# Fourth PV of a chunk directly behind gate/up, W2 tiles fetched six ahead, and another order of the first half's output projection

## The chip, the cores and the metric

The kernel runs on one core of a Trainium2 chip. The metric is the time of one execution on the device in microseconds (us). Before the change it is 560.99 us, the median of three runs (560.61, 560.99, 562.88).

## What is computed

Layer normalisation, then attention and a gated feed-forward layer side by side on the same normalised rows, and the sum of both with the input:

```
xn = layernorm(x)                                   # 2048 x 576
q, k, v = heads of xn @ wqkv                        # 32 heads of 18
p = softmax(q k^T / sqrt(18)), key within the 256 last positions
a = (p v) @ wo
h = silu(xn @ w1) * (xn @ w3)                       # 2048 x 4608
out = x + a + h @ w2
```

## The kernel before

The 2048 rows go in four chunks of 512 (`c` = 0 to 3). A chunk has three stages on TensorE.

1. For chunks 1 to 3, nine projection jobs make q, k and v (for chunk 0 they stand ahead of everything).
2. Thirty-six gate/up units (`u` = 0 to 35). Unit `u` makes 128 of the 4608 hidden columns for all 512 rows with 18 matmuls on 64 rows each, nine pairs (`unit_pairs`, line 686). Its up and gate results stand in two banks of PSUM. ScalarE takes tanh of the gate bank (`unit_tanh`, line 695), and VectorE makes the hidden tile in two instructions (`unit_h`): line 701 reads the gate bank, line 704 the up bank. Between units stand the score steps (line 570) with their exponentials on ScalarE (579) and masks on GpSimd (606), spaced by a count of matmul pairs (`clock`, `nxt`), and three of the four PV groups (`pv`, line 627), each for eight heads. VectorE is also given the statistics and the normalisation (lines 371 to 383) of the next chunk's rows; those of its last 128 rows stand at units 33 and 35 (`near`).
3. The W2 stage. The output has two halves of 288 columns. Per half, nine tiles of W2 (512 x 288, 288 KB) are each used by 16 matmuls of 128 rows (line 744), four row tiles `tt` by four `fl`; the four accumulators `ACC[tt]` are PSUM banks. The attention output is projected into the same accumulators: first the remainder, four matmuls on 64 rows (`wr`, line 756), later the others (`wo`, line 750). At the end of half 0, VectorE adds x and stores each accumulator (`out`, line 764), and SP sends it off (766). The order is a list (`p2_list`), its items counted by `n`, which starts at -4 with the four remainder matmuls.

PSUM has eight banks. The units take three pairs in turn, scores the fourth. In the W2 stage the accumulators are the pair of unit 33 and the score pair; the fourth PV group takes the two banks of unit 34, since `ring_of` begins with `jobs[NF - 2]`. Its results go over VectorE (line 636, transposes), a reciprocal (641), a scaling on GpSimd (642), VectorE again (649) and four transfers on SP (`o_pack`, line 674) into `oT`, from which `wo` reads. GpSimd also copies the old keys (`keep_keys`, line 550) at the head of the stage.

The queues work in program order. SP issues most transfers: the gate/up weights (`w13`, three buffers, each filled by six parts of 192 KB, `load_part`, line 323; `owed` hands them out two per unit, each behind a named TensorE instruction), x rows (299), the transposed normalised rows (408), and the exchange of their halves (`xn_swap`, line 415, into `xnS`). ACT's queue issues the W2 tiles (`load_w2`, line 355). There are eight W2 buffers: four of their own, and four (`w2x`) in the gate/up buffer that the last units have read. Tiles 0 to 3 of the next chunk are fetched in the W2 stage of this one (`next_w2`); for chunk 0 they are fetched by SP at units 20, 22, 24 and 26.

The kernel waits by semaphores that a small dependency tracker (`_Prog`) places: a first write to a bank waits for all readers of what stood in it.

Of the kernel before, what the change touches and what calls it, by code (L numbers as in the profile page):

```python
# [164 lines left out]
def bass_parallel_sum__sliding_block__glu_gated_swiglu__prompt_kernel(  # L165
# [18 lines left out]
    NC = S // CH  # L184
    TB = CH // 128
    G = H // 4
    NF = F // 128
    NFC = F // 512
# [9 lines left out]
    with ExitStack() as es:  # L198
# [1 line left out]
        def sb(name, shape, dtype=dt.bfloat16):  # L200
            return es.enter_context(nc.sbuf_tensor(name, shape, dtype))

        NXP, NOF, NPT, NW13, NW2, NOD = 7, 4, 10, 3, 4, 2
        KB, NB, NV = 64, CH // 64, 12
        ident = sb("ident", [128, 128])
        xp = [sb(f"xp{i}", [128, D]) for i in range(NXP)]
# [10 lines left out]
        wo = sb("wo", [128, 5, D])  # L217
        w13 = [sb(f"w13_{i}", [128, 9, 512]) for i in range(NW13)]
        w2 = [sb(f"w2_{i}", [128, 4, HD]) for i in range(NW2)]
# [36 lines left out]
        oT = sb("oT", [128, 5, CH])  # L256
# [26 lines left out]
        def half_bank(b):  # L283
# [5 lines left out]
            out=ident[:], in_=ident[:], compare_op=ALU.not_equal, fill=1.0,  # L289
# [5 lines left out]
        def load_x(t, eng="sp"):  # L295
            nonlocal xp_ctr
            s = xp_ctr % NXP
            xp_ctr += 1
            add(eng, lambda e: e.dma_start(xp[s][:], x2[t * 128:(t + 1) * 128, :]), w=[("xp", s)], dma=f"xp{s}")
            return s  # L300
# [11 lines left out]
        def load_part(after=(), behind=()):  # L312

            nonlocal nfill
            if nfill >= 6 * NC * NFC:
                return
            k, i = divmod(nfill, 6)
            s, dst = w13_at(k)
            part, n = divmod(i, 2)
            c0 = (k % NFC) * 512  # L320
            src = (B_w3, B_w1)[n]
            nfill += 1
            add("sp", lambda e: e.dma_start(
                dst[64 * n:64 * n + 64, 3 * part:3 * part + 3, :],
                src[192 * part:192 * part + 192, c0:c0 + 512].rearrange("(kd p) f -> p kd f", p=64)),
                r=list(behind), after=after, dma=f"w13_{s}_{n}", **{"j" if i else "w": [("w13", s)]})
# [5 lines left out]
        def last_pe():  # L332
            return next(o for o in reversed(P.ops) if o.eng == "pe")
# [6 lines left out]

        w2x = w13[1][:, :, :].rearrange("p a b -> p (a b)")[:, 0:NW2 * 4 * HD].rearrange("p (n k d) -> p n k d", n=NW2, d=HD)

        def w2_at(c, i):
            n = i % (2 * NW2)
            if n < NW2:
                s = (n + 2 * c) % NW2
                return s, w2[s]
            return n, w2x[:, n - NW2, :, :]

        def load_w2(c, i, eng="act", after=()):  # L350
            if c >= NC:
                return
            s, dst = w2_at(c, i)
            half, fc = divmod(i, NFC)
            add(eng, lambda e: e.dma_start(
                dst[:, :, :], B_w2[fc * 512:(fc + 1) * 512, half * HD:(half + 1) * HD].rearrange("(fl p) d -> p fl d", p=128)),
                w=[("w2", s)], after=after, dma=f"w2_{s}")

        def next_w2(c, i):
            if i < 10:  # L360
                load_w2(c, i + 8)
            elif i < 12:
                load_w2(c + 1, i - 10)
            elif i >= 16:
                load_w2(c + 1, i - 14)


        def ln_stats(t, s, part):
# [340 lines left out]
        def p2_list(c):  # L709

            seq = []
            for half in range(2):
                apart = half == 0 or c + 1 < NC
                if half == 0:
                    seq += [("wr", 0, 0, 0, tt, 0, False) for tt in range(TB)]
                for fc in range(NFC):
                    sl = half * NFC + fc
                    edge = fc == NFC - 1 or (half == 1 and fc == 0)
                    pairs = [(fl, tt) for fl in range(4) for tt in range(TB)]
                    if edge:  # L720
                        pairs = [(fl, tt) for tt in range(TB) for fl in range(4)]
                    for n, (fl, tt) in enumerate(pairs):
                        seq.append(("w2", half, fc, fl, tt, sl, n == len(pairs) - 1))
                        if fc == NFC - 1 and fl == 3:
                            seq += [("wo", half, fc, kd, tt, sl, False) for kd in range(4 if apart else 5)]
                            if half == 0 or not apart:
                                seq.append(("out", half, fc, 0, tt, sl, False))
            if c + 1 < NC:
                for what in ("wr", "out"):
                    seq += [(what, 1, 0, 0, tt, 0, False) for tt in range(TB)]  # L730
            return seq
# [3 lines left out]
        def p2_item(c, item, xs):  # L735
            nonlocal of_ctr
            what, half, fc, k, tt, sl, last = item
            d0 = half * HD
            bank = PS[:, ACC[tt], 0:HD]
            key = [("ps", ACC[tt])]  # L740
            if what == "w2":
                f = fc * 4 + k
                buf, wt = w2_at(c, sl)
                add("pe", lambda e: e.matmul(  # L744
                    bank, hT[:, f, tt * 128:(tt + 1) * 128], wt[:, k, :], start=(f == 0 and half == 1), stop=False),
                    r=[("h", f), ("w2", buf)], **{"w" if f == 0 and half == 1 else "j": key})
                if last:
                    next_w2(c, sl)
            elif what == "wo":
                add("pe", lambda e: e.matmul(  # L750
                    bank, oT[:, k, tt * 128:(tt + 1) * 128], wo[:, k, d0:d0 + HD], start=False,
                    stop=(k == (3 if half == 0 else 4))),
                    r=[("oT", j) for j in range(G // 2)] + ["oTz", "wo"], j=key)
            elif what == "wr":
                r0 = 64 * (tt % 2)
                add("pe", lambda e: e.matmul(  # L756
                    bank, oT[r0:r0 + 64, 4, tt * 128:(tt + 1) * 128], wo[r0:r0 + 64, 4, d0:d0 + HD],
                    start=(half == 0), stop=(half == 1), tile_position=(r0, 0)),
                    r=[("oT", 0), "oTz", "wo"], **{"w" if half == 0 else "j": key})
            else:  # L760
                o = of_ctr % NOF
                of_ctr += 1
                t = c * TB + tt
                add("dve", lambda e: e.tensor_tensor(ofin[:, o, :], bank, xp[xs[tt]][:, d0:d0 + HD], ALU.add),  # L764
                    r=key + [("xp", xs[tt])], w=[("of", o)])
                add("sp", lambda e: e.dma_start(out2[t * 128:(t + 1) * 128, d0:d0 + HD], ofin[:, o, :]),
                    r=[("of", o)], dma=f"out{o}")
# [67 lines left out]
        for h in range(2):  # L835
# [9 lines left out]
            for n, (dst, src) in enumerate(moves):  # L845
                dealt.append(add("pool", lambda e, dst=dst, src=src: e.tensor_copy(dst, src),
                                 r=[f"wqk{h}", "wqkd"], **{"j" if n else "w": [f"wp{h}"]}))
# [30 lines left out]
        for c in range(NC):  # L878
# [21 lines left out]
            side = {}  # L900
# [48 lines left out]
            for u in range(NF):  # L949
# [13 lines left out]
                    if n in (3, 8):  # L963
                        owe_part(op)
                unit_tanh(u, b0[0])
                if u % 4 == 3 and u < NF - 4 and (c or u != 15):
                    owed += 6
                if next_pv in pv_ready and clock >= pv_ready[next_pv] and next_pv < 3:
                    j = next_pv
# [38 lines left out]
                if c == 0 and u == 18:  # L1008
# [3 lines left out]
                    for p in range(2):  # L1012
                        add("sp", lambda e, p=p: e.dma_start(wo[64 * p:64 * p + 64, 4, :], rows[:, 2:Dh, :]),
                            j=["wo"], dma="wo")
                if c == 0 and u in (20, 22, 24, 26):
                    load_w2(0, (u - 20) // 2, "sp")
                if u == 29:
                    xs = [load_x(c * TB + tt) for tt in range(TB)]
            assert done == len(att) and next_pv == 3, (done, next_pv)
            ring_of[:] = [*jobs[NF - 2], *jobs[NF - 1]]  # L1020
# [3 lines left out]
            if c + 1 < NC:  # L1024
                for g in range(G):
                    keep_keys(g)
            for i in range(NW2, 2 * NW2):
                load_w2(c, i, after=(last_pe(),))
            banks = ()
            for n, item in enumerate(p2_list(c), -TB):  # L1030
                p2_item(c, item, xs)
                if n == 3:
                    for u in sorted(side):
                        for what in side.pop(u):
                            what()
                elif n == 19:
                    banks = (ring(), ring())
                    pv(c, 3, banks)
                    pv_out(banks[0], 0)
                    pv_out(banks[1], 1)  # L1040
                    o_scale(0)
                    o_turn(6, 0)
                    o_turn(6, 1)
                    o_scale(1)
                    o_turn(7, 0)
                    o_turn(7, 1)
                    o_pack(3, "sp")
                elif n == 40 and c + 1 < NC:
                    xn_send((c + 1) * TB + 3)
                elif n == 300 and c + 1 < NC:  # L1050
                    xn_swap(c + 1, ("sp", "sp"))
                elif n in (100, 120) and c + 2 < NC:
                    t = (c + 2) * TB + (n == 120)
                    xslot[t] = load_x(t)

        with nc.Block() as block:
            P.replay(es, block)
# [28 lines left out]
```

## Time and profile before

| What | Value |
|---|---|
| median of 3 runs | 560.99 us |
| profiled execution, its own time | 560.94 us |
| its span | 559.1 us |
| TensorE matmul busy | 554.5 us (99%) |
| VectorE / ScalarE / GpSimd busy | 311.8 / 253.0 / 163.4 us |
| gate/up matmuls (line 686) | 181.9 + 154.9 us busy |
| W2 matmuls (line 744) | 147.3 us busy, 1152 of them |
| bytes moved by DMA | 85.90 MB, mean 154 GB/s |

The span is the time between the first and the last instruction of the profiled execution. An instruction's row in the order of time has its start in the span, its length, its engine and line, the tiles it writes and reads, and how many of its kind follow one another; square brackets hold the engine's idle time before it and who ended it. A matmul's length includes its way through the array, so that rows of one engine overlap; the distance from start to start is what a matmul costs.

### The profile page before, as it was taken

To read this page: it belongs to the slowest core of one execution; us is meant where nothing else is said; L and a number is where in the kernel's file an instruction comes from. 1 tells how busy PE (TensorE), PEld (TensorE's weight loads), DVE (VectorE), ACT (ScalarE), POOL (GpSimd) and SP (SyncE) were. 2 spreads that over 40 slices of the span, in tenths; PEclk is the share of its full clock that TensorE was granted. 3 is DMA by queue.
4 is the path that set the end of the run, shared out by engine and by line. 5 is a ranking of instruction groups with operands and counts; after the bars stand their busy time and mean duration, and the time that the engine had idled before them with its cause. 6 is when DMAs were issued, how large, how long until landed. Compare 5 with 4: busy or idle time off the path is not lost.

```text
span 559.1 us, 15730 instructions
## 1 busy us (share of the span) xinstructions
PE 554.5 (99%) x6767; PEld 346.9 (62%) x6767; DVE 311.8 (56%) x584; ACT 253.0 (45%) x349; POOL 163.4 (29%) x383
## 2 busy tenths in 40 slices
PE   9999999999999999999999999999999999999998
PEld 4445455677687455477766545547777654555776
DVE  7466788710366778851046668884105567767211
ACT  4357776100286776600037777650004676666000
POOL 6413454400033445330003444533000333433000
PEclk9999999999999999999999999999999999999999
DMA  9998899994366368599325736869913673661730
GB/s 249 206 192 183 186 187 193 213 266 122 86 141 146 89 175 161 138 238 258 86 72 138 167 86 160 162 172 243 228 51 74 137 172 95 150 163 32 203 107 22
DMA packets 127883, 85.90 MB, mean 154 GB/s; under 512 B 35430, under 2 KB 125502, under 8 KB 127814
## 3 DMA queue, kind: packets, MB, share of 16 engines
q1 hardware_dynamic: 89890, 63.17, 50.6%
q10 hardware_dynamic: 37924, 21.73, 16.0%
q8 instruction: 53, 0.87, 0.7%
q14 instruction: 16, 0.13, 0.1%
HBM read 71.37 MB, written 2.36 MB: 132 GB/s over the span
## 4 chain that ended last, share of the span: by engine, by line
PE 95%; DMA 2%; DVE 1%; SPq 0%; POOL 0%; issue 0%
PE ps L686 50%; PE ps L744 23%; PE ps L450 9%; PE ps L570 6%; PE ps L627 4%; PE ps L750 3%; DMA oT<-od 1%; DMA xp<-in_A_x_dram 0%; SPq L674 0%; PE ps L756 0%; DVE xn L383 0%; POOL oq L642 0%; DVE od L649 0%; DVE stats L371 0%; DVE stats L373 0%
## 5 line engine op out<-in xcount | busy, mean ns | idle before, releaser
L686 PE MATMUL ps<-xnT,w 64*128 64x512 bf16 x1400 | 181.9, 376 | 0.0
L686 PE MATMUL ps<-xnS,w 64*128 64x512 bf16 x1120 | 154.9, 376 | 0.0
L744 PE MATMUL ps<-w,hT 128*128 128x288 bf16 x1152 | 147.3, 286 | 0.1
L701 DVE SCALAR_TENSOR_TENSOR gs<-th,ps 128x512 bf16<-128x512 bf16 x144 | 97.8, 680 | 80.3 <-ACT th L695 78.9
L579 ACT ACTIVATE pt<-ps 128x1024 bf16<-128x1024 f32 (+1 forms) x112 | 113.2, 1011 | 63.4 <-PE ps L570 62.4
L744 PEld LDWEIGHTS ps<-w,hT 128*128 128x128 bf16 x1152 | 112.0, 98 | 29.9 <-issue 1.5
L686 PEld LDWEIGHTS ps<-xnT,w 64*128 64x128 bf16 x1400 | 72.5, 94 | 56.3
L606 POOL TENSOR_TENSOR pt<-pt,mk 128x128 int32<-128x128 int32 (+1 forms) x199 | 80.5, 427 | 79.3 <-ACT pt L579 79.3
L704 DVE SCALAR_TENSOR_TENSOR hT<-gs,ps 128x512 bf16<-128x512 bf16 x144 | 98.9, 686 | 5.0
L695 ACT ACTIVATE th<-ps 128x512 bf16<-128x512 f32 x144 | 85.4, 593 | 23.8 <-PE ps L686 23.6
L686 PEld LDWEIGHTS ps<-xnS,w 64*128 64x128 bf16 x1120 | 59.0, 94 | 51.1
L764 DVE TENSOR_TENSOR ofin<-ps,xp 128x288 bf16<-128x288 f32 x32 | 13.8, 454 | 121.9 <-PE ps L750 63.8
L463 ACT ACTIVATE stage<-ps 128x512 bf16<-128x512 f32 x16 | 9.6, 597 | 145.1 <-PE ps L450 142.8
L606 POOL TENSOR_TENSOR hT<-hT,mk 128x128 int32<-128x128 int32 (+1 forms) x31 | 12.4, 422 | 168.5 <-ACT hT L579 168.5
L570 PE MATMUL ps<-qv,kv 64*128 64x320 bf16 (+4 forms) x528 | 53.5, 260 | 0.0
L570 PEld LDWEIGHTS ps<-qv,kv 64*128 64x128 bf16 x528 | 28.0, 94 | 25.1 <-ACT pt L579 0.5
L450 PE MATMUL ps<-xnT,wp 64*128 64x512 bf16 (+1 forms) x360 | 39.0, 355 | 0.0
L579 ACT ACTIVATE stage<-ps 128x1024 bf16<-128x1024 f32 x24 | 24.6, 1024 | 12.6 <-PE ps L570 12.6
L649 DVE STREAM_TRANSPOSE od<-oq 128x256 bf16<-128x256 bf16 x64 | 25.8, 427 | 6.3 <-POOL oq L642 6.3
L450 PEld LDWEIGHTS ps<-xnT,wp 64*128 64x128 bf16 x360 | 20.0, 94 | 13.1
L642 POOL TENSOR_TENSOR oq<-uq,rden 128x288 bf16<-128x288 f32 x16 | 10.8, 674 | 39.0 <-DVE rden L641 39.0
L606 POOL TENSOR_TENSOR stage<-stage,mk 128x128 int32<-128x128 int32 (+1 forms) x42 | 17.0, 423 | 17.3 <-ACT stage L579 17.2
(60 smaller groups left out, 353.0 us busy)
## 6 DMA issues: line engine op xcount, KB each, us to landing
w<-in_B_w_dram SPq DMA_DIRECT2D x210, 192.0 KB, 4.3
w<-in_B_w_dram ACTq DMA_DIRECT2D x68, 288.0 KB, 5.7
xp<-in_A_x_dram SPq DMA_DIRECT2D x29, 144.0 KB, 5.0
out_dram<-ofin SPq DMA_DIRECT2D x32, 72.0 KB, 2.0
xnS<-xnT SPq DMA_DIRECT2D x8, 256.0 KB, 5.2
oT<-od SPq DMA_DIRECT2D x56, 36.0 KB
pt<-in_A_wqkv_dram SPq DMA_DIRECT2D x4, 288.0 KB, 6.5
hT<-in_B_w_dram SPq DMA_DIRECT2D x6, 192.0 KB, 7.3
```

The lines of the kernel that those rows point to most:

```text
L450: op = add("pe", lambda e, out_=out_, st=st, mv=mv, n=n, r0=r0, first=first: e.matmul(out_, st, mv, start=first, stop=(part == 1 and n == ...
L570: add("pe", lambda e, r0=r0, out_=out_, kb=kb, q0=q0, nb=nb: e.matmul(out_, kb4[r0:r0 + 64, g, kb + NV - NB, :] if kb < 0 else kv[r0:r0 + ...
L579: add("act", lambda e: e.activation(pt_slot(sl)[:, 0:w, :], PS[:, SC[0]:SC[1] + 1, 0:w].rearrange("p r q -> p q r"), ACT.Exp, scale=scale) ...
L606: add("pool", lambda e, vb=vb, mm=mm: e.tensor_tensor(vb, vb, mm, ALU.mult), r=(key if n == 0 else []) + ["mk"], **{"w" if n == 0 else "j" ...
L627: add("pe", lambda e, p=p, q=q, pr=pr, sl=sl, g=g, pos=pos, q0=q0, nb=nb, col=col, first=first, n=n: e.matmul(PS[32 * q:32 * q + VW, banks ...
L649: add("dve", lambda e: e.transpose(od[i][:, g % 2, c0:c0 + CH // 2], oq[:, c0:c0 + CH // 2]), r=["oq", "oq0"], **{"j" if half or g % 2 els ...
L686: op = add("pe", lambda e, n=n, r0=r0, r=r, k=k, src=src: e.matmul(PS[:, b0 + r, :], wt[r0:r0 + 64, k, fl * 128:(fl + 1) * 128], src, star ...
L695: add("act", lambda e: e.activation(th[i][:], PS[:, bg, :], ACT.Tanh, scale=0.5), r=[("ps", bg)], w=[("th", i)])
L701: add("dve", lambda e: e.scalar_tensor_tensor(out=gs[i][:], in0=th[i][:], scalar=1.0, in1=PS[:, bg, :], op0=ALU.add, op1=ALU.mult), r=[("t ...
L704: add("dve", lambda e: e.scalar_tensor_tensor(out=hT[:, u, :], in0=gs[i][:], scalar=0.5, in1=PS[:, bu, :], op0=ALU.mult, op1=ALU.mult), r= ...
L744: add("pe", lambda e: e.matmul(bank, hT[:, f, tt * 128:(tt + 1) * 128], wt[:, k, :], start=(f == 0 and half == 1), stop=False), r=[("h", f ...
L750: add("pe", lambda e: e.matmul(bank, oT[:, k, tt * 128:(tt + 1) * 128], wo[:, k, d0:d0 + HD], start=False, stop=(k == (3 if half == 0 else ...
```

## The change

- **PV.** The fourth PV group with its whole chain up to `o_pack(3)` stands at `n == -1`, right behind the four remainder matmuls and before the first W2 matmul, not behind the twentieth W2 matmul (`n == 19`).
- **W2 tiles.** Tile `i` lies in buffer `i` mod 8 in every chunk. When tile `i` is used up in the order, tile `i + 6` is put into ACT's queue (before, `i + 8`, which goes into the buffer just read). Tiles 4 and 5 are fetched at the head of the stage (before, 4 to 7). Tiles 0 to 3 are fetched by SP at units 20, 22, 24 and 26 in every chunk.
- **Other transfers.** The six gate/up parts that were handed out behind unit 31 are issued one by one in the second half of the W2 stage (`n` = 170 to 295), each behind the TensorE instruction at its place. The four loads of x rows for the addition move from unit 29 to unit 31.
- **Half 0's projection.** All 144 W2 matmuls come first, then two projection matmuls for each row tile (`k` = 0, 1, which wait only for packed groups 0 to 2), then per row tile the other two and its addition. Before, each row tile had its last four W2 matmuls, four projection matmuls and its addition in turn.

```
-        NXP, NOF, NPT, NW13, NW2, NOD = 7, 4, 10, 3, 4, 2
+        NXP, NOF, NPT, NW13, NW2, NOD, AHEAD = 7, 4, 10, 3, 4, 2, 6
...
-        def w2_at(c, i):
+        def w2_at(i):
             n = i % (2 * NW2)
-            if n < NW2:
-                s = (n + 2 * c) % NW2
-                return s, w2[s]
-            return n, w2x[:, n - NW2, :, :]
+            return n, w2[n] if n < NW2 else w2x[:, n - NW2, :, :]
...
-        def next_w2(c, i):
-            if i < 10:
-                load_w2(c, i + 8)
-            elif i < 12:
-                load_w2(c + 1, i - 10)
-            elif i >= 16:
-                load_w2(c + 1, i - 14)
...
-                        if fc == NFC - 1 and fl == 3:
+                        if fc == NFC - 1 and fl == 3 and half == 1:
                             seq += [("wo", half, fc, kd, tt, sl, False) for kd in range(4 if apart else 5)]
-                            if half == 0 or not apart:
+                            if not apart:
                                 seq.append(("out", half, fc, 0, tt, sl, False))
+                if half == 0:
+                    seq += [("wo", 0, 0, kd, tt, 0, False) for tt in range(TB) for kd in range(2)]
+                    for tt in range(TB):
+                        seq += [("wo", 0, 0, kd, tt, 0, False) for kd in (2, 3)] + [("out", 0, 0, 0, tt, 0, False)]
...
                 if last:
-                    next_w2(c, sl)
+                    if sl + AHEAD < 2 * NFC:
+                        load_w2(sl + AHEAD)
...
-                    r=[("oT", j) for j in range(G // 2)] + ["oTz", "wo"], j=key)
+                    r=[("oT", j) for j in range(3 if half == 0 and k < 2 else G // 2)] + ["oTz", "wo"], j=key)
...
-                if u % 4 == 3 and u < NF - 4 and (c or u != 15):
+                if u % 4 == 3 and u < NF - 8 and (c or u != 15):
                     owed += 6
...
-                if c == 0 and u in (20, 22, 24, 26):
-                    load_w2(0, (u - 20) // 2, "sp")
-                if u == 29:
+                if u in (20, 22, 24, 26):
+                    load_w2((u - 20) // 2, "sp")
+                if u == 31:
                     xs = [load_x(c * TB + tt) for tt in range(TB)]
...
-            for i in range(NW2, 2 * NW2):
-                load_w2(c, i, after=(last_pe(),))
+            for i in range(NW2, AHEAD):
+                load_w2(i, after=(last_pe(),))
...
-                if n == 3:
-                    for u in sorted(side):
-                        for what in side.pop(u):
-                            what()
-                elif n == 19:
+                if n == -1:
+                    assert not side
                     banks = (ring(), ring())
                     pv(c, 3, banks)
...
+                elif n in (170, 195, 220, 245, 270, 295) and c + 1 < NC:
+                    load_part((last_pe(),))
```

More of the change, by code (lines that the diff above doesn't have):

```diff
@@ L341, in bass_parallel_sum__sliding_block__glu_gated_swiglu__prompt_kernel, with load_w2 @@
         w2x = w13[1][:, :, :].rearrange("p a b -> p (a b)")[:, 0:NW2 * 4 * HD].rearrange("p (n k d) -> p n k d", n=NW2, d=HD)
-        def w2_at(c, i):
+        def w2_at(i):
             n = i % (2 * NW2)
-            if n < NW2:
-                s = (n + 2 * c) % NW2
-                return s, w2[s]
-            return n, w2x[:, n - NW2, :, :]
[L350 to L353, printed above, removed]
+            return n, w2[n] if n < NW2 else w2x[:, n - NW2, :, :]
+        def load_w2(i, eng="act", after=()):
+            s, dst = w2_at(i)
             half, fc = divmod(i, NFC)
@@ L742, in p2_item @@
                 f = fc * 4 + k
-                buf, wt = w2_at(c, sl)
+                buf, wt = w2_at(sl)
                 add("pe", lambda e: e.matmul(
```

## The prediction

> **What bounds the kernel now.** I read the page's busy shares first, then the chain of waits, then the order of time around the start of a W2 stage, engine by engine. Page, parts 1, 2 and 4:
>
> ```profile
> PE 554.5 (99%) x6767; PEld 346.9 (62%) x6767; DVE 311.8 (56%) x584; ACT 253.0 (45%) x349; POOL 163.4 (29%) x383
> ...
> PEclk9999999999999999999999999999999999999999
> DMA  9998899994366368599325736869913673661730
> ...
> PE 95%; DMA 2%; DVE 1%; SPq 0%; POOL 0%; issue 0%
> ```
>
> TensorE is busy everywhere, its granted clock is full in all forty slices, and 95% of the chain that ended last is its own work. Its work is the same before and after: every matmul is kept. So the change can move only what stands between matmuls, and that is little. The order of time of TensorE, chunk 0, from the last gate/up unit on:
>
> ```profile
> 101.76 0.41 PE L756 MATMUL ps<-wo,oT 64*128 64x288 bf16 x4
> 102.10 2.62 PE L744 MATMUL ps<-w,hT 128*128 128x288 bf16 x20
> 104.65 1.07 PE L627 MATMUL ps<-pt,va 64*20 64x320 bf16 x72
> 105.66 13.89 PE L744 MATMUL ps<-w,hT 128*128 128x288 bf16 x112
> 120.00 0.65 PE L750 MATMUL ps<-wo,oT 128*128 128x288 bf16 x4 [0.45 <-DMA oT<-od]
> 120.48 0.65 PE L744 MATMUL ps<-w,hT 128*128 128x288 bf16 x4
> ```
>
> The reader is to see three things: the fourth PV (L627) stands 2.55 us behind the start of W2; the change of tile shape costs a little each time; and one wait for the packed attention output (oT) at 120.00, in this chunk alone. VectorE beside it:
>
> ```profile
> 101.46 0.63 DVE L701 SCALAR_TENSOR_TENSOR gs<-th,ps 128x512 bf16<-128x512 bf16 x1
> 102.12 0.69 DVE L704 SCALAR_TENSOR_TENSOR hT<-gs,ps 128x512 bf16<-128x512 bf16 x1
> 102.73 0.68 DVE L701 SCALAR_TENSOR_TENSOR gs<-th,ps 128x512 bf16<-128x512 bf16 x1
> 103.44 0.69 DVE L704 SCALAR_TENSOR_TENSOR hT<-gs,ps 128x512 bf16<-128x512 bf16 x1
> 104.05 0.98 DVE L383 TENSOR_SCALAR xn<-xp,mv,rstd 128x576 bf16<-128x576 bf16 x2
> 105.79 0.72 DVE L636 STREAM_TRANSPOSE uq<-ps 128x512 f32<-128x512 f32 x1 [0.76 <-PE ps L627]
> ```
>
> The first pair is unit 34, the second unit 35. VectorE is behind: unit 34 leaves its up bank only at 102.12 + 0.69 = 102.81, when W2 has long begun. Today nobody feels it. Chunk 1, the same place:
>
> ```profile
> 239.61 0.41 PE L756 MATMUL ps<-wo,oT 64*128 64x288 bf16 x4
> 239.95 2.62 PE L744 MATMUL ps<-w,hT 128*128 128x288 bf16 x20
> ```
>
> and VectorE there, unit 34:
>
> ```profile
> 239.79 0.69 DVE L704 SCALAR_TENSOR_TENSOR hT<-gs,ps 128x512 bf16<-128x512 bf16 x1
> ```
>
> **The change part by part.** The sum is made against the profiled execution: 560.94 us, span 559.1, 1.84 outside the span. The median of the runs shown is 560.99, so the two differ by 0.05.
>
> *PV(3) moved ahead of W2.* It writes the two banks of unit 34 (`ring()` starts with `jobs[NF - 2]`), its first matmul the up bank, so it can't start before that unit's hT is done. Today twenty W2 matmuls cover this; afterwards only the four remainder matmuls (L756) stand between, and these end the cover at the moment when W2 starts today. From VectorE's end to a waiting TensorE I take 0.06 us: at the kernel's start the normalised rows end at 8.81 + 0.64 = 9.45 and the transpose (L395) that waits for them starts at 9.51. So TensorE stands still
> - chunk 0: 102.81 + 0.06 - 102.10 = 0.77
> - chunk 1: 240.48 + 0.06 - 239.95 = 0.59
> - chunk 2 (hT ends 377.22 + 0.69 = 377.91, W2 starts 377.38): 0.59
> - chunk 3 (514.86 + 0.69 = 515.55, against 515.10): 0.51
>
> Sum +2.46. Behind the waiting PV on TensorE lies all of W2, so nothing hides it. The scores' last mask is no second wait: POOL ends it at 98.88 in chunk 0 and 514.15 in chunk 3. PV's evacuation (L636) sits on VectorE behind unit 35 and the normalisation that ends at 105.03, so it comes only some 0.8 us earlier in chunk 0; POOL's copies of old keys (102.46 to 105.34) still precede the scaling, which is wanted after 106. The four packing transfers move with PV on SP, past the two x loads and the transposed rows only as before, and no longer behind w13 parts.
>
> *Fewer changes of tile shape.* Twenty W2 matmuls between the remainder and PV take 104.65 - 102.10 = 2.55 us; the 112 of chunk 1 take 257.54 - 243.81 = 13.73, 0.1226 each, which makes 2.45 for twenty. The 0.098 between is what one more change of tile shape costs: today the order is remainder, W2, PV, W2 (three changes), afterwards remainder, PV, W2 (two). Four times: -0.39; were it hidden in PV's wait, 0.
>
> *Output projection of half 0 reordered.* Today chunk 0's 112 matmuls should end at 105.66 + 13.73 = 119.39, and the projection starts at 120.00: 0.61 lost to oT. Afterwards the first projection matmul that reads group 3 stands behind all 144 W2 matmuls and eight projection matmuls (2.45 us later in the order), and the packing starts earlier. -0.61. The other chunks show no such wait.
> The new order has its price: the four additions (L764) that free the accumulators now come within six matmuls of the second half. An addition starts 0.32 us after the last projection matmul's start and ends 0.46 later (120.37 to 120.69 to 121.15), so with the 0.06 the bank is free 0.84 after; the second half asks for it after seven matmul steps, 7 x 0.1226 = 0.86. Later tiles are safe: VectorE does four additions in 1.55 us, 0.36 apart, and TensorE asks every 0.49. So the price is between nothing and, if the waiting matmul's weight load of 0.098 us can't run ahead, 0.08 per chunk. At 120.00 today the weight load did start with the release, so I take 0.05, four times: +0.20; ends 0 and +0.32.
> The Trainium skill, "TensorE: Matmul & The Clock Gate", Step-by-step and "LDWEIGHTS (loading the stationary operand)", says that weight loads are pulled ahead of matmuls in flight and last columns / 1.2 ns; as an estimate from that page an exposed load of 128 columns is 107 ns, and this term would be 0.09 per chunk, the total 562.76 instead of 562.60.
>
> *Transfers.* Per chunk 14 W2 tiles stay on ACT with the same moments: tile i + 8 still can't be issued before tile i is read, since eight buffers exist, and ACT computes nothing in this stage. For chunks 1 to 3 tiles 0 to 3 move from ACT, late in the W2 stage before, to SP at units 20 to 26: twelve issues of 0.60 us on SP (its row in chunk 0), with 288 KB each. Chunk 0 already has just this, with DMA busy at 9 tenths, and TensorE does not wait there. In chunk 1 (by the view of stretches, DMA busy 0.67 and 0.82 in 196 to 210 and 210 to 224) the transfers that feel it are the w13 parts behind them on SP: the last part for unit 32 is issued at 221.01 and landed at 225.69, unit 32 starts at 231.6 (four units of 1.94 and one score step of 0.22 ahead of the remainder at 239.61), so 5.9 us are in hand. Three tiles ahead of it are 0.86 MB, 4.3 us at the 200 GB/s of a full stretch (163 GB/s at 0.82), less what drains in SP's waits. Cost 0.
> The six w13 parts that leave units 32 to 34 (192 KB each) go to the second half of W2, where DMA is at 0.46 and 0.31 (126 to 140 and 266 to 280). Each makes SP wait for a W2 matmul. Behind them on SP queues the exchange of halves for the next chunk (xnS), issued at 124.55 today, at about 142 afterwards; it lands 5.2 us later, near 147, and the first unit reads it at 157.0. Cost 0; without this cover, each us of lateness would be one of TensorE. The x rows at unit 31 instead of 29 are first added 18 us later: 0.
>
> Sum: 2.46 - 0.39 - 0.61 + 0.20 = +1.66, so **562.60**, 0.3% above before. What a measurement here can tell from no change is about 0.5%, 2.8 us.
>
> **The rivals.**
> *PV finds its bank free.* If unit 34 left it before the fourth remainder matmul, only the gains stay: 560.94 - 0.39 - 0.61 = 559.94. For it: the gate bank is free at 102.09, in time. Against it: PV's first matmul writes the up bank, 0.45 to 0.72 later in all four chunks.
> *The second half waits for its accumulators.* If VectorE's additions come later than in today's rows, each half boundary loses, say, one more addition of 0.46 instead of 0.05: 562.60 - 0.20 + 4 x 0.46 = 564.24. It decides from 0.02 us of delay on; for it speaks this thin margin, against it that VectorE is idle for 10 us before.
> *W2 tiles on SP delay gate/up weights* (the slower side of no change). In the W2 stage of chunk 0 a tile issued at 105.02 landed at 117.12, 12.1 us, when both queues were full. With that in unit 32 of chunks 1 to 3, issued about 1.4 later: 222.4 + 12.1 = 234.5, 2.9 us late, three times: 571.3. It decides from a landing of 9.2 us on. Against it: with the same queueing in chunk 0 parts took 3.5 to 6.7.
> The Trainium skill, "DMA: Bandwidth & Descriptors", Queues, rings and completion order, says that one issuer's descriptors are consumed in ring order while rows of different issuers alternate; by that rule the tiles moved to SP stand ahead of the parts instead of beside them. The long times for W2 above show queueing, not which rule makes it.
>
> **How the numbers follow.** Forecast 0.70, its own range 561.7 to 563.5 (the terms' ends, and a halt of 0.24 at 387.62 in chunk 2 with no cause shown). Bank free 0.09, accumulators 0.08, late weights 0.10, something unseen that gains 0.03. The range from 559.9 to 564.6 takes in the first three, 0.87. Faster by over 0.5% (below 558.2): 0.03. Slower (above 563.8): 0.10 + 0.08 + 0.05 of the forecast's upper tail = 0.23. Within: 0.74.
>
> **What would show it.** TensorE's first PV row of each group at hT's end of unit 34 plus 0.06, 0.5 to 0.8 us behind L756's end of cover; no wait for oT in chunk 0; the second half following the projection with at most 0.1 us between; no wait for w or xnS. A TensorE wait on a weight transfer, or a PV start without a gap, makes the forecast wrong.

## The result and the profile after

The changed kernel takes 562.76 us (median of 14 runs, 562.38 to 563.52), the kernel before 561.12 (14 runs beside it). The ratio is 1.0027, with a 95% interval of 1.002 to 1.0035: slower by a quarter of a per cent, below the 0.5% bound used in the prediction. The forecast was 562.6. The profiled execution took 562.52 us, its span is 560.8; against the execution before (560.94) that is 1.58 us more. One run in the experiments below, of the kernel with the transfers alone, took 3325.29 us where its ten others took 560.12 to 561.52; its cause is open, and its ratio leaves it out.

The page of the changed kernel, its span and busy time, the granted clock, and the shares of the chain that ended last (L673 is the gate/up unit now, L735 W2, L614 PV, L691 the hT instruction):

```profile
span 560.8 us, 15730 instructions
...
PE 553.8 (99%) x6767; PEld 349.9 (62%) x6767; DVE 310.5 (55%) x584; ACT 253.0 (45%) x349; POOL 163.0 (29%) x383
...
PEclk9999999999999999999999999999999999999999
...
PE 93%; DVE 4%; issue 1%; ACT 1%; DMA 1%; POOL 0%; ACTq 0%
```

As many TensorE instructions as before, the same clock, but VectorE has gone from 1% of the chain to 4%: TensorE's work now hangs on VectorE's at some place. TensorE's order of time at the W2 stage of chunk 0 names it:

```profile
101.99 0.41 PE L748 MATMUL ps<-wo,oT 64*128 64x288 bf16 x4
103.10 1.07 PE L614 MATMUL ps<-pt,va 64*20 64x320 bf16 x72 [0.70 <-DVE hT L691]
104.10 17.82 PE L735 MATMUL ps<-w,hT 128*128 128x288 bf16 x144
121.75 2.12 PE L742 MATMUL ps<-wo,oT 128*128 128x288 bf16 x16
123.78 2.49 PE L735 MATMUL ps<-w,hT 128*128 128x288 bf16 x19
```

and VectorE's beside it (unit 34's pair, and the four additions at the end of half 0):

```profile
101.70 0.63 DVE L688 SCALAR_TENSOR_TENSOR gs<-th,ps 128x512 bf16<-128x512 bf16 x1
102.36 0.69 DVE L691 SCALAR_TENSOR_TENSOR hT<-gs,ps 128x512 bf16<-128x512 bf16 x1
...
123.18 1.55 DVE L756 TENSOR_TENSOR ofin<-ps,xp 128x288 bf16<-128x288 f32 x4 [13.33 <-PE ps L742]
```

PV begins 0.05 us after unit 34's hT (102.36 + 0.69 = 103.05). There is no wait for oT at the projection any more. From the first of the 16 projection matmuls to W2 again are 123.78 - 121.75 = 2.03 us, where sixteen steps of 0.1226 are 1.96: the 0.07 is the second half's wait for its first accumulator.

A count over the whole profiled execution, from the starts of the matmuls, accounts for the difference. The last matmul starts 1.71 us later than before (557.80, 556.08).

| Part | us |
|---|---|
| gaps from remainder to PV, four chunks: 0.984, 0.801, 0.801, 0.709, each less the 0.215 that the passage to W2 took before | +2.44 |
| wait for oT in chunk 0 (a step of 0.733 before, 0.122 now) | -0.61 |
| start of the second halves, 0.193 instead of 0.123, four times | +0.28 |
| halt in chunk 2 at 387.6, without a cause in the profile, not there in this execution | -0.24 |
| first gate/up matmul (22.19, before 21.98) and the units of chunk 0 | +0.24 |
| what is left: one change of tile shape fewer in each chunk | -0.39 |
| sum (the parts are rounded) | +1.71 |

### The profile page after: what moved, and what is told of

Same layout as the page of the kernel before. It is cut to its first block, busy times and chain, and to the rows that moved or that the text cites. A ratio compares the mean times of both kernels' runs of the same rounds, so it can differ in the third digit from the quotient of the medians.

```text
span 560.8 us, 15730 instructions
## 1 busy us (share of the span) xinstructions
PE 553.8 (99%) x6767; PEld 349.9 (62%) x6767; DVE 310.5 (55%) x584; ACT 253.0 (45%) x349; POOL 163.0 (29%) x383
## 4 chain that ended last, share of the span: by engine, by line
PE 93%; DVE 4%; issue 1%; ACT 1%; DMA 1%; POOL 0%; ACTq 0%
PE ps L673 46%; PE ps L735 25%; PE ps L437 9%; PE ps L557 6%; PE ps L614 4%; PE ps L742 3%; DVE hT L691 1%; DVE gs L688 1%; DMA xp<-in_A_x_dram 1%; DVE stats L358 0%; DVE stats L360 0%; ACT th L682 0%; DVE xn L370 0%; DVE mv L361 0%; ACT pt L566 0%
## 5 line engine op out<-in xcount | busy, mean ns | idle before, releaser
L673 PE MATMUL ps<-xnT,w 64*128 64x512 bf16 x1400 | 182.3, 376 | 0.0
L673 PE MATMUL ps<-xnS,w 64*128 64x512 bf16 x1120 | 155.2, 376 | 0.0
L735 PE MATMUL ps<-w,hT 128*128 128x288 bf16 x1152 | 144.4, 286 | 0.0
L735 PEld LDWEIGHTS ps<-w,hT 128*128 128x128 bf16 x1152 | 112.1, 98 | 29.3 <-issue 0.9
L673 PEld LDWEIGHTS ps<-xnT,w 64*128 64x128 bf16 x1400 | 73.7, 94 | 55.3
L691 DVE SCALAR_TENSOR_TENSOR hT<-gs,ps 128x512 bf16<-128x512 bf16 x144 | 98.9, 687 | 5.0
L673 PEld LDWEIGHTS ps<-xnS,w 64*128 64x128 bf16 x1120 | 60.2, 94 | 50.0 <-issue 0.2
L437 PE MATMUL ps<-wv,xnT 64*128 64x288 bf16 x288 | 21.7, 283 | 0.1
```

Source lines behind the costliest of these rows:

```text
L437: op = add("pe", lambda e, out_=out_, st=st, mv=mv, n=n, r0=r0, first=first: e.matmul(out_, st, mv, start=first, stop=(part == 1 and n == ...
L673: op = add("pe", lambda e, n=n, r0=r0, r=r, k=k, src=src: e.matmul(PS[:, b0 + r, :], wt[r0:r0 + 64, k, fl * 128:(fl + 1) * 128], src, star ...
L691: add("dve", lambda e: e.scalar_tensor_tensor(out=hT[:, u, :], in0=gs[i][:], scalar=0.5, in1=PS[:, bu, :], op0=ALU.mult, op1=ALU.mult), r= ...
L735: add("pe", lambda e: e.matmul(bank, hT[:, f, tt * 128:(tt + 1) * 128], wt[:, k, :], start=(f == 0 and half == 1), stop=False), r=[("h", f ...
```

## The experiments

All ratios are to the kernel before, timed beside each experiment on the same chip; its medians there were 561.05 to 561.22 us. A ratio is not the quotient of the two medians: in one experiment below it is 1.0000 where the medians are 0.5 us apart. So differences of a few tenths of a us are read from the traces here, not from the times.

### PV put back, and PV moved alone

In the changed kernel:

```
-                if n == -1:
+                if n == 19:
```

> The changed kernel with its fourth PV put back behind the twentieth W2 matmul; transfers and the order of half 0's projection as changed. Theory (the change loses its time where PV waits for unit 34's bank: 0.77 + 0.59 + 0.59 + 0.49 = 2.44 us of gaps in the changed trace, less 0.39 for one change of tile shape fewer): the gaps between the remainder and PV vanish, the time falls by about 2.05 us from the changed kernel, to 0.3 us below the kernel before (ratio 0.9994). Rival (the moved transfers cost the time): it stays at about 1.6 us above the kernel before (1.0027).

Measured 560.59 us, ratio 0.9989 (0.998 to 0.9999). No step between matmuls over 0.3 us is left at this place; the four steps of 0.193 at the second halves stay. The counterpart, in the kernel before:

```
-                if n == 3:
-                    for u in sorted(side):
-                        for what in side.pop(u):
-                            what()
-                elif n == 19:
+                if n == -1:
+                    assert not side
```

> The kernel before with the fourth PV alone moved ahead of W2. Theory: gaps of 0.77, 0.59, 0.59 and 0.5 us ahead of PV, and no wait for oT in chunk 0, since packing comes 0.75 us earlier and is wanted some 0.7 us later: 2.44 - 0.39 - 0.61 = +1.44 us, ratio 1.0026. Rival (transfers cost the time): about the time before less 1.0 (0.998).

Measured 562.53 us, ratio 1.0025 (1.0016 to 1.0035). The gaps are 0.986, 0.802, 0.802 and 0.713, and the wait for oT is gone. Chunk 0 (in this kernel the lines have the numbers of the kernel before):

```profile
101.67 0.41 PE L756 MATMUL ps<-wo,oT 64*128 64x288 bf16 x4
102.78 1.05 PE L627 MATMUL ps<-pt,va 64*20 64x320 bf16 x72 [0.70 <-DVE hT L704]
```

So the move of PV alone makes the whole loss, and without it the rest of the change gains a little.

### PV in the banks of unit 35

```
-            ring_of[:] = [*jobs[NF - 2], *jobs[NF - 1]]
+            ring_of[:] = [*jobs[NF - 1], *jobs[NF - 2]]
```

> The changed kernel with one edit: the fourth PV takes the banks of unit 35 instead of unit 34, which VectorE leaves 1.32, 1.37, 1.37 and 1.46 us later. Theory (PV's start is set by the reader of its bank): the four gaps grow by 5.5 us together, the time to about 568.1 (ratio 1.0125), PV starting 0.055 us after unit 35's hT. Rival (the gaps come from the change of tile shape or from the masks): the time stays at the changed kernel's (1.0027).

Measured 569.04 us (four runs, 568.17 to 571.29), ratio 1.0142 (1.0116 to 1.0169). The profiled execution, at 568.17, is 0.1 from the 568.1 expected; the median of the four is 0.9 above it, and why they spread over 3 us is not known. Order of time of TensorE and of VectorE, chunk 0:

```profile
101.89 0.41 PE L748 MATMUL ps<-wo,oT 64*128 64x288 bf16 x4
104.32 1.05 PE L614 MATMUL ps<-pt,va 64*20 64x320 bf16 x72 [2.02 <-DVE hT L691]
```

```profile
103.58 0.69 DVE L691 SCALAR_TENSOR_TENSOR hT<-gs,ps 128x512 bf16<-128x512 bf16 x1
```

103.58 + 0.69 = 104.27 is the end of unit 35's hT, and PV starts 0.05 later. The gaps are 2.307, 2.175, 2.177 and 2.168, together 5.53 more than in the changed kernel. Neither the tile shape nor the masks changed here; the reader of the bank decides.

### PV at the same place, its wait taken away

```
-            ring_of[:] = [*jobs[NF - 2], *jobs[NF - 1]]
+            ring_of[:] = [*job(), *jobs[NF - 1]]
             ring_ctr = 0
-            ACC[:] = [*job(), *SC]
+            ACC[:] = [*SC, *job()]
...
-                if n == -1:
+                if n == -3:
```

> The changed kernel with the fourth PV in the banks of unit 33, which are free in time, between the second and the third remainder matmul; two accumulators take unit 34's banks instead, and the remainder matmuls that write them come behind PV. What PV waits for is taken away, not PV's place. Theory: no gap of over 0.35 us ahead of PV, 2.44 us less, and about 0.1 per chunk more for one more change of tile shape: the changed kernel less 2.05, which is 0.3 below the kernel before (ratio 0.9994). Rival (PV so early loses time in itself, by its place): within 0.5 of the changed kernel (1.0027).

Measured 560.52 us, ratio 0.9993 (0.9984 to 1.0002). All four steps into PV are 0.21. PV loses nothing by standing early; it lost by the bank. The second kernel of this kind also changes the order of half 0's projection:

```
-                    seq += [("wo", 0, 0, kd, tt, 0, False) for tt in range(TB) for kd in range(2)]
                     for tt in range(TB):
-                        seq += [("wo", 0, 0, kd, tt, 0, False) for kd in (2, 3)] + [("out", 0, 0, 0, tt, 0, False)]
+                        seq += [("wo", 0, 0, kd, tt, 0, False) for kd in range(4)] + [("out", 0, 0, 0, tt, 0, False)]
```

> As the kernel with PV in unit 33's banks, and half 0's projection goes row tile by row tile, four matmuls and the addition, still behind all W2 matmuls. The second half then asks for its first accumulator twelve projection matmuls later. Theory: the gaps of 0.193 us where the second half starts fall to the usual 0.123, 0.07 per chunk, 0.28 in all; oT is in time (packed at 117.5 in chunk 0 of the changed kernel, wanted at about 121): 0.6 below the kernel before (0.9989). Rival: the gap is a fixed cost of starting an accumulator anew and stays.

Measured 560.18 us, ratio 0.9983 (0.9975 to 0.9992): faster than both kernels, and the lowest median here (that it is faster than the other experiments near 560.5 us is not shown). TensorE, chunk 0 (L747 the remainder, L734 W2):

```profile
101.97 0.29 PE L747 MATMUL ps<-wo,oT 64*128 64x288 bf16 x2
102.18 1.05 PE L614 MATMUL ps<-pt,va 64*20 64x320 bf16 x72
103.16 0.30 PE L747 MATMUL ps<-wo,oT 64*128 64x288 bf16 x2
103.39 3.85 PE L734 MATMUL ps<-w,hT 128*128 128x288 bf16 x30
```

Remainder, PV, remainder and W2 follow each other without an idle time. The steps into the second half are 0.122 in all four chunks, so the 0.07 was a wait and no fixed cost of starting an accumulator.

### The order of the projection alone, and the transfers alone

In the kernel before, `p2_list` and the read set of `wo`:

```
-                        if fc == NFC - 1 and fl == 3:
+                        if fc == NFC - 1 and fl == 3 and half == 1:
...
+                if half == 0:
+                    seq += [("wo", 0, 0, kd, tt, 0, False) for tt in range(TB) for kd in range(2)]
+                    for tt in range(TB):
+                        seq += [("wo", 0, 0, kd, tt, 0, False) for kd in (2, 3)] + [("out", 0, 0, 0, tt, 0, False)]
...
-                    r=[("oT", j) for j in range(G // 2)] + ["oTz", "wo"], j=key)
+                    r=[("oT", j) for j in range(3 if half == 0 and k < 2 else G // 2)] + ["oTz", "wo"], j=key)
```

> The kernel before with the order of half 0's projection alone changed. Theory: the wait for oT in chunk 0 (0.61 us) goes, and four gaps of 0.07 us come at the start of the second halves: -0.33 us (0.9994).

Measured 560.72 us, ratio 1.0000 (0.9991 to 1.0008): the timing can't tell 0.33 us from nothing. The trace can: the wait for oT is gone, and the second halves start after 0.193, 0.191, 0.193 and 0.194. Half 0's end in chunk 0, L754 the projection, L748 W2:

```profile
121.03 2.12 PE L754 MATMUL ps<-wo,oT 128*128 128x288 bf16 x16
123.06 2.12 PE L748 MATMUL ps<-w,hT 128*128 128x288 bf16 x16
```

It is the same 2.03 us from start to start as in the changed kernel.

The transfers alone are the changed kernel with that same edit taken back and PV behind twenty W2 matmuls:

```
-                        if fc == NFC - 1 and fl == 3 and half == 1:
+                        if fc == NFC - 1 and fl == 3:
...
-                if half == 0:
-                    seq += [("wo", 0, 0, kd, tt, 0, False) for tt in range(TB) for kd in range(2)]
...
-                if n == -1:
+                if n == 19:
```

> The kernel before with the transfers alone as changed (W2 tiles 0 to 3 on SP at units 20 to 26 in every chunk, six ahead in the stage, gate/up parts in the second half, x rows at unit 31). Theory (transfers are hidden): no wait for a weight; oT of chunk 0 may land early enough to take away the wait of 0.61 us, since six parts no longer stand beside it: between -0.61 and 0 us (0.999 to 1.000). Rival (the transfers cost): above 1.001.

Measured 560.47 us, ratio 0.9991 (0.9981 to 1.0000). TensorE waits for no transfer of a gate/up or W2 weight in the profile, and not for oT either: with the six parts out of the way it lands in time. In this kernel L731 is W2 and L738 the projection:

```profile
105.83 13.89 PE L731 MATMUL ps<-w,hT 128*128 128x288 bf16 x112
119.56 0.65 PE L738 MATMUL ps<-wo,oT 128*128 128x288 bf16 x4
```

112 steps of 0.1226 end at 119.56, just where the projection starts. So the wait for oT was removed by three parts of the change, each by itself: PV earlier, the later projection, and the lighter queue.

### How much cover the moved transfers leave

```
+                if c and u in (18, 20, 22):
+                    load_w2((u - 16) // 2, "sp")
                 if u in (20, 22, 24, 26):
                     load_w2((u - 20) // 2, "sp")
```

Tiles 1, 2 and 3 are fetched twice here.

> The changed kernel with three more transfers of 288 KB on SP at units 18, 20 and 22 of chunks 1 to 3: tiles 1, 2 and 3 of W2 are fetched twice. It prices the cover that the moved transfers use up: in the changed trace the last part for unit 32 of chunk 1 lands at 230.04 and the unit starts at 231.98, so 1.9 us are left (5.9 before). If the cover is what I take it for, 0.86 MB more ahead of that part bring it some 4 to 5 us later: TensorE waits 2 to 3.5 us for a weight part at unit 32 in chunks 1 and 2 and little in chunk 3, in all 5 to 8 us (568 to 571). If SP's waits or spare DMA time absorb it, the time stays at the changed kernel's 562.8.

Measured 564.88 us (four runs, 563.13 to 565.88), ratio 1.0059 (1.0036 to 1.0082): 2.1 us more than the changed kernel, less than half of what I expected. The view of waits:

```profile
PEld ps L673 <- DMA w<-in_B_w_dram: 2.1, 2, 1.3
PE ps L673 <- DMA w<-in_B_w_dram: 1.1, 1, 1.1
```

and TensorE at the start of unit 32 of chunk 1 (233.00; the pair before it is unit 31's last):

```profile
232.09 0.38 PE L673 MATMUL ps<-xnT,w 64*128 64x512 bf16 x2
233.00 1.04 PE L673 MATMUL ps<-xnT,w 64*128 64x512 bf16 x8 [0.53 <-issue]
```

The steps at unit 32 are 0.91 and 1.44 in chunks 1 and 2, against 0.22 in the usual case, so the weights cost 1.9 us. Chunk 3 has a step of 0.58 too, but not at unit 32, and the profile names no transfer for it; it comes back in a later experiment without these transfers. The place was right. The size was not: the last part for unit 32 of chunk 1 landed at 232.91 where it had landed at 230.04, 2.9 us later instead of 4 to 5. So the moved transfers are hidden, but three more tiles on this queue are not; as an estimate from 2.9 us for three, two would use up the 1.9 us of cover.

### Why VectorE is late at unit 34

The third question was whether the wait could be mended at its source. First theory: three instructions of statistics at unit 33.

```
-            near = {0: (20, 22, 23), 1: (24, 26, 27), 2: (30, 32, 33), 3: (33, 35, 40)}
+            near = {0: (20, 22, 23), 1: (24, 26, 27), 2: (30, 32, 33), 3: (31, 35, 40)}
```

> The changed kernel with one edit: the statistics of the next chunk's last 128 rows stand at unit 31 instead of unit 33 on VectorE. It asks why unit 34 leaves its bank late. Theory: in chunks 0 to 2 these three instructions (1.0 us) push unit 34's pair back; with them away the pair follows the tanh and ends 0.6 to 0.8 us earlier, so the three gaps of 0.77, 0.59 and 0.59 shrink to at most 0.1 each, while chunk 3, which has no such statistics and waits for its tanh behind an exponential, keeps 0.49. The changed kernel less 1.7 to 1.95 us, level with the kernel before (ratio 0.9995 to 1.000). Rival (VectorE is late by its whole load near the end of the units, not by these three): all four gaps stay within 0.2 of what they are, 1.0027.

Measured 561.94 us, ratio 1.0016 (1.0007 to 1.0025). The gaps are 0.892, 0.478, 0.479 and 0.712: they shrank by 0.09, 0.32 and 0.32 and not to nothing, together by 0.74, and the time fell by 0.8. VectorE of this kernel, chunk 0, up to unit 34:

```profile
99.78 0.64 DVE L370 TENSOR_SCALAR xn<-xp,mv,rstd 128x576 bf16<-128x576 bf16 x2
100.33 0.67 DVE L688 SCALAR_TENSOR_TENSOR gs<-th,ps 128x512 bf16<-128x512 bf16 x1
101.04 0.69 DVE L691 SCALAR_TENSOR_TENSOR hT<-gs,ps 128x512 bf16<-128x512 bf16 x1
101.65 0.68 DVE L688 SCALAR_TENSOR_TENSOR gs<-th,ps 128x512 bf16<-128x512 bf16 x1
102.36 0.69 DVE L691 SCALAR_TENSOR_TENSOR hT<-gs,ps 128x512 bf16<-128x512 bf16 x1
```

No row has a wait: VectorE works off a backlog, and what was taken out was filled from behind. The theory fell, and so did its rival, by which no gap would move by more than 0.2. A kernel built on it, with the projection row tile by row tile and, in chunk 3 alone, PV in unit 33's banks, fell with it:

> The same, with half 0's projection row tile by row tile, and in chunk 3 alone the fourth PV in unit 33's banks. Theory: the four waits for PV and the four gaps of 0.07 at the second halves are gone, and chunks 0 to 2 keep one change of tile shape fewer than the kernel before: 562.5 - 2.44 - 0.28 + 0.1 = 559.9 (ratio to the kernel before 0.998), some 0.3 below the kernel with PV in unit 33's banks everywhere. Rival (the statistics moved ahead delay other work of VectorE that TensorE waits for): not below 560.2.

Measured 561.60 us, ratio 1.0007 (0.9998 to 1.0016); the gaps of chunks 0 to 2 are 0.888, 0.479 and 0.473 as above, chunk 3 has none, and the second halves start without a gap (0.122 and 0.123).

Second theory: the backlog of units 31 to 34. The normalisation of 256 rows goes further ahead.

```
-            near = {0: (20, 22, 23), 1: (24, 26, 27), 2: (30, 32, 33), 3: (33, 35, 40)}
+            near = {0: (20, 22, 23), 1: (24, 26, 27), 2: (26, 28, 29), 3: (28, 30, 40)}
```

> The changed kernel with the normalisation of the next chunk's last 256 rows moved further ahead on VectorE: statistics at units 26 and 28, application at units 28 and 30 (before 30 and 33, and 32 and 35). In the changed trace VectorE has not one wait between 91 and 105 us, so taking one group of three instructions away at unit 33 only drew the backlog after it. Theory (unit 34 leaves its bank late because VectorE carries a backlog through units 31 to 34): with 3 us less there, the backlog is gone before unit 34, the gaps ahead of PV in chunks 0 to 2 fall below 0.1 us beyond the usual step, chunk 3 keeps 0.49: 1.7 to 1.95 us less than the changed kernel, ratio 0.9993 to 1.000. Rival (the pair itself and its tanh take that long after unit 34 ends): gaps as with the statistics at unit 31 (0.68, 0.26, 0.26), ratio 1.0016.

Measured 562.75 us, ratio 1.0028 (1.0018 to 1.0038). The gaps did what the theory says: 0.229, 0.302, 0.298 and, in chunk 3, 0.708. In chunk 0, PV follows the remainder at once:

```profile
102.11 0.41 PE L748 MATMUL ps<-wo,oT 64*128 64x288 bf16 x4
102.46 1.05 PE L614 MATMUL ps<-pt,va 64*20 64x320 bf16 x72
```

But the time didn't fall. TensorE now waits for VectorE in the units, in chunk 1 and the same way in chunk 2:

```profile
230.97 0.38 PE L673 MATMUL ps<-xnT,w 64*128 64x512 bf16 x2
231.94 0.82 PE L673 MATMUL ps<-xnT,w 64*128 64x512 bf16 x6 [0.59 <-DVE hT L691]
```

The steps are 0.965 and 0.961, 1.5 us more than usual together, and chunk 3, whose VectorE order is untouched, has one of 0.589 for which the profile names no releaser. The kernel with three more tiles had that step (0.577) at the same place, 14.66 us ahead of its PV. The shift also moved the spacing of the score steps, which `near` feeds; what of the new wait comes from the one and what from the other was not tried. So the backlog as the cause of the lateness is shown for chunk 0. In chunks 1 and 2 TensorE's own halt, 0.75 us more than the usual step and 8.65 us ahead of PV, also gave VectorE time; that VectorE then waited 0.45 and 0.96 us for a tanh in chunk 1, more than the halt, speaks for the backlog there, but the two were not separated. Moving that work about is no remedy: the wait came back elsewhere. Chunk 3's 0.49 has no normalisation in it; by the order of time before, its tanh stands behind an exponential (its gs waited 0.54 for the tanh). That was not tried.

## Why the prediction was right

**What bounds the kernel.** Right: the same number of matmuls at the same clock, and the whole difference between matmuls.

**PV moved ahead of W2.** Predicted 0.77, 0.59, 0.59, 0.51, in all 2.46; measured 0.77, 0.59, 0.59, 0.49, in all 2.44. The 0.06 from VectorE's end to TensorE's start was 0.054 to 0.055 in all four chunks. The experiment with unit 35's banks shows the cause, not only the size.

**Fewer changes of tile shape.** Predicted -0.39, left over in the count above as -0.39; that is a remainder, not a measurement. In the trace before, the passages from the remainder to W2 and from W2 to PV are steps of 0.215 and 0.216 where W2 has 0.123, so one passage fewer in four chunks makes 0.37. With unit 33's banks one change is given back, and that kernel comes out level with the one that has PV at its old place (560.52 and 560.59).

**The projection's order.** The 0.61 went, as predicted, though the order was not needed for it: the transfers alone or PV's place alone remove it too. The prediction had the w13 parts only ahead of the packing on SP; that the changed transfers by themselves would bring oT in time it did not say.

**The second half's accumulators.** Predicted 0.05 per chunk (row by row 0 to 0.08), measured 0.07: a term mis-sized by 0.08 us in all. The estimate from the Trainium skill ("TensorE: Matmul & The Clock Gate", LDWEIGHTS) was 0.09. The measured value lies between, nearer to neither; a weight load that can't run ahead is what fits (in chunk 0 the load starts at 123.753, 0.03 ahead of its matmul, while the loads behind it start 0.12 ahead of theirs), and the row tile by row tile order removes it.

**Transfers.** No wait for a weight, as predicted, and the exchange of halves was issued at 140.85 where 142 was said and landed at 145.8, long before the first unit reads it. The cover shrank from 5.9 to 1.9 us (landed 230.04, unit 32 at 231.98): the part landed 4.35 us later than before (225.69), 1.84 of it by a later issue and 2.5 by a longer flight. That is all of the 4.3 that the prediction took as the most it could be; what it hoped would drain in SP's waits was nothing. The rival's point of decision, a landing of 9.2 us after issue, was not reached: that part took 7.2.

**The rivals.** PV did not find its bank free: its step is 0.71 to 0.98. The accumulators cost 0.07, not 0.46. The weights were not late here, and were with three tiles more. Whether one issuer's ring order, as the Trainium skill ("DMA: Bandwidth & Descriptors", Queues, rings and completion order) has it, or the common engines held them back, no run here shows.

**What was not in the sum.** A halt of 0.24 in the one execution before, and 0.2 in the kernel's start; they cancel in this pair of executions. That is luck: with either of them alone the total would have been 0.2 us off. The forecast is right by its parts, which the trace and the experiments show one by one; the closeness of the sum says less, since the runs of the changed kernel alone lie 1.1 us apart.

## What to carry to other kernels

Before moving work up in a kernel whose bounding engine is full, look up which buffer it writes and when the last reader of that buffer ends in the trace: the end of that row, plus the release, is when the moved work starts, and everything behind it waits. If another buffer is free at that time, give it that one; here it took the whole cost away, while emptying the late reader's queue only moved the wait. And where a wait is gone, check whether another part of the same change had removed it already.

## What was not expected of the hardware

From the end of VectorE's hT to PV's start were 0.054 to 0.057 us in sixteen starts of four kernels (the changed one, PV moved alone, unit 35's banks, statistics at unit 31), as at the kernel's start (0.06): a price that held to a hundredth of a us. Three further transfers of 288 KB on one queue put a part back by 2.9 us and not by the 4.3 that the bytes at 200 GB/s make, while the three moved there by the change put it back by 4.35.

And halts of TensorE between two ordinary matmuls stand in the profile without a releaser: 0.24 in the execution before, and 0.36 and 0.37 at one place of chunk 3 in two experiments. The traces hold one thing that goes with them. There are 53 transfers of instructions of 16 KB on queue 8 of the page, one for each 257 of the 13622 instructions that the trace shows of TensorE. In these three runs one such transfer started late, at 385.31, 502.09 and 499.93, which is 496, 466 and 482 of TensorE's instructions behind the one before it, the longest distance in each run; the halt ended 2.7 to 2.9 us after that start. That speaks for instructions that came late. It is not shown: distances of 474 and 484 stand in other runs without such a halt, and no experiment changed them.
